# Two Abs, and two Exp, as one operation over a two-bank PSUM tile in the filter generation of a fused adaLN, S4D and Mixer kernel

## The chip, the core and the metric

The kernel runs on one core of a Trainium2 chip. A core has five engines that run side by side, each through its own instructions in order: TensorE (PE, matrix products into PSUM), VectorE (DVE), ScalarE (ACT, activation functions), GpSimd (POOL) and SyncE (SP, which here only starts transfers). They wait for each other through semaphores. The metric is the device time of one execution in microseconds, here the median of the runs shown.

## The reference

The block has two branches with adaptive layer norms. The first is a diagonal state space layer (S4D): for each of 448 channels a filter of 2048 taps is generated from 256 complex states and applied as a long convolution. The second is a token-mixing MLP.

```python
dt = jnp.exp(log_dt)
A = -jnp.exp(log_A_real) + 1j * A_imag
C = (C_real + 1j * C_imag) * dt[:, None]
P = jnp.exp((A * dt[:, None])[:, :, None] * pos[None, None, :])
K = 2.0 * jnp.einsum("dn,dnl->dl", C, P).real
...
y = jnp.fft.irfft(Uf * Kf[None, :, :], L2)[:, :, :L]
...
h = _layernorm(x, axis=-1) * (1 + ca) + sa
x = x + ga * _A_ref(h, ...)
h = _layernorm(x, axis=-1) * (1 + cb) + sb
x = x + gb * _B_ref(h, ...)
```

`_B_ref` is layer norm, a product with `w1` over the 2048 tokens, GELU and a product with `w2` back to the tokens, for each of the 448 channels.

## The kernel before

The kernel has three stages: parameters of the states; the filters together with the convolution (as a two-stage discrete Fourier transform); the token MLP. The change is in the filters.

A tap's position is split into a coarse part of 32 values and a fine part of 64, so that a state's contribution is a product of two factors, E over the fine part and G over the coarse part. The sum over states then is a matrix product that contracts the states: `kg` (line 684). A group is 16 channels, so there are 28 groups; the 256 states are taken in two halves of 128, one on each partition. A half group is one such half of one group, and there are 56, numbered `s`.

Each half group needs magnitudes and angles. Both are computed by PE from small factors into PSUM, in two tiles of 128 x 512 floats, `xe` (for E) and `xg` (for G), each as large as one PSUM bank. `st_exponents` (line 611) makes the exponents, and `st_exp` (616) turns them into magnitudes by one Exp for each tile. `st_phase` (622) makes the phases in turns, by four matmuls for each tile: a product, two that add and subtract a large constant so as to round to whole turns, and a product that leaves the fraction. The helper `halves` (605) issues each matmul twice, for `xe` with the first 64 rows of the PE array and for `xg` with the last 64.

`st_step` (641) uses them. On ACT it takes Abs of `xe` into `ab` and Abs of `xg` into `cg_`, then four Sin: of `xe` in place (652), of `xg` into `sg` (653), of `cg_` in place as the cosine (654), and of `ab` into `xg`, also a cosine (655). POOL multiplies `sg` and `cg_` with the magnitudes into G (657, 658). DVE multiplies `xe` and `xg` with magnitudes into E (659 and 660, and after the work of `between`, 662 and 663). `st_mag2` (633, on POOL) makes the magnitudes of the second half of the fine part.

Exp and Sin need different function tables on ACT, and a table is loaded anew at each switch. So the half groups are taken in seven batches of eight: `window` (978) makes the eight Exp of a batch, then eight steps make the Sin.

The order of PE, ACT, DVE and POOL is written out by hand: each runs its instructions in the order of the source. In step `s`, `st_phase(s + 1)` is issued ahead of `st_step(s)`, so PE works one step ahead. For `s` below 32, `st_kgen(s - 2)` (675) goes ahead of the phases; above 32, `st_kgen(s - 1)` goes behind them. Between these lies the work of the convolution: before the 32nd half group that of the input (`u_rows`, `u_cols`), later `pc_s2`, `pc_mul`, `pc_inv`, `pc_out` of the first half of the channels. Its copies out of PSUM are put into the lists `dve` and `act` and issued in `between` and behind the step.

Buffers are reused in turn, and an instruction that writes into a reused buffer waits for the last reader of the tile that was there. `xe` and `xg` come from the pool `pph` with two buffers each, four banks in all. In SBUF `ab` has one buffer of 512 floats on each partition; `sg` and `cg_` share the tag `gs` with three.

Of the kernel before, what the change touches and what calls it, by code (L numbers as in the profile page):

```python
# [11 lines left out]
F32 = mybir.dt.float32  # L12
F32R = mybir.dt.float32r
BF16 = mybir.dt.bfloat16
AF = mybir.ActivationFunctionType
# [7 lines left out]
P = 128  # L23
# [11 lines left out]
TWO_PI = 6.283185  # L35
# [187 lines left out]
def tile_adaln_s4d_mixer(ctx, tc, i, out):  # L223
# [20 lines left out]
    with ExitStack() as es:  # L244
        V, S, G, T = nc.vector, nc.scalar, nc.gpsimd, nc.tensor
# [10 lines left out]
        cg, mp, wp = right("cg", 1), right("mp", 8), right("wp", 2)  # L256
        m2p = [right("m2", 3)]
        pms = es.enter_context(tc.tile_pool(name="pms", bufs=3, space=PSUM))
        pph = kgen.enter_context(tc.tile_pool(name="pph", bufs=2, space=PSUM))
# [71 lines left out]
        for q in range(4):  # L331
            r = slice(32 * q, 32 * q + 1)
# [149 lines left out]
        def modulation(k, *halves):  # L482
            if 0 in halves:
                pmods[k] = pms.tile([P, D], F32, tag="ms", name="pm")
            for h in halves:
                for q in (2 * h, 2 * h + 1):
                    T.matmul(pmods[k], scb[:, q], wms[k][:, q], start=q == 0, stop=q == 3)
            if 1 not in halves:
                return
            pm = pmods.pop(k)  # L490
            act.append(lambda: S.activation(mod[k], pm, AF.Copy, bias=1.0 if k in (1, 4) else 0.0))
# [4 lines left out]
        nm = xp.tile([P, 16], F32, name="nm")  # L496
# [87 lines left out]
        mags, m2s, eg, phs = {}, {}, {}, {}  # L584
# [20 lines left out]
        def halves(out, lhs, rhs, start, stop):  # L605

            for k in range(2):
                r = slice(64 * k, 64 * k + 64)
                T.matmul(out[k], lhs[r], rhs[r], start=start, stop=stop)  # L609

        def st_exponents(s):
            g, h = divmod(s, 2)
            phs[s] = [pph.tile([P, 512], F32, tag=nm, name=nm) for nm in ("xe", "xg")]
            halves(phs[s], lex[g % 4][:, h * P : (h + 1) * P], tab[:, 2], True, True)

        def st_exp(s):
            mags[s] = mp.tile([P, 2, 512], F32, tag="mag", name="mag")
            pm = phs.pop(s)
            for k in range(2):
                S.activation(mags[s][:, k], pm[k], AF.Exp)  # L620

        def st_phase(s):

            g, h = divmod(s, 2)
            lhs = lph[g % 3][:, h * P : (h + 1) * P]
            pm = [pph.tile([P, 512], F32, tag=nm, name=nm) for nm in ("xe", "xg")]
            halves(pm, lhs, tab[:, 1], True, False)
            halves(pm, mg[:, 0], ones, False, False)
            halves(pm, mg[:, 1], ones, False, False)
            halves(pm, lhs, tab[:, 0], False, True)  # L630
            phs[s] = pm
# [9 lines left out]
        def st_step(s, between):  # L641
            me, mg_, m2 = v32(mags[s][:, 0]), v32(mags[s][:, 1]), m2s.pop(s)
            E = gp_.tile([P, 2, GD, NJ], F32, tag="E", name="E")
            Gt = gp_.tile([P, 2, GD, NI], F32, tag="G", name="G")


            xe, xg = phs.pop(s)
            ab, sg, cg_ = (wp.tile([P, 512], F32, tag=nm, name=nm, bufs=b) for nm, b in (("ab", 1), ("gs", 3), ("gs", 3)))

            S.activation(ab, xe, AF.Abs)  # L650
            S.activation(cg_, xg, AF.Abs)
            S.activation(xe, xe, AF.Sin, scale=TWO_PI)  # L652
            S.activation(sg, xg, AF.Sin, scale=-TWO_PI)  # L653
            S.activation(cg_, cg_, AF.Sin, scale=-TWO_PI, bias=math.pi / 2)  # L654
            S.activation(xg, ab, AF.Sin, scale=-TWO_PI, bias=math.pi / 2)  # L655
            se, ce = v32(xe), v32(xg)
            G.tensor_tensor(Gt[:, 1], mg_, v32(sg), ALU.mult)  # L657
            G.tensor_tensor(Gt[:, 0], mg_, v32(cg_), ALU.mult)  # L658
            V.tensor_tensor(E[:, 1, :, 32:64], m2, se, ALU.mult)  # L659
            V.scalar_tensor_tensor(E[:, 1, :, 31::-1], me[:, :, 31::-1], -1.0, se, ALU.mult, ALU.mult)  # L660
            between()
            V.tensor_tensor(E[:, 0, :, 31::-1], me[:, :, 31::-1], ce, ALU.mult)
            V.tensor_tensor(E[:, 0, :, 32:64], m2, ce, ALU.mult)  # L663
            eg[s] = (E, Gt)
            mags.pop(s)
# [312 lines left out]
        def window(s):  # L978
# [7 lines left out]
            if s == 0:  # L986
                st_exponents(s)
            for e in range(BATCH):
                st_exp(s + e)

                if e + 1 < BATCH:
                    st_exponents(s + e + 1)
                else:
                    st_phase(s)
# [45 lines left out]
        for s in range(tail):  # L1040
# [23 lines left out]
            def between():  # L1064
                flush(dve)
                if s == 9:
                    tt(mod[0], mod[0], mod[2], ALU.mult)
                if 2 <= s < BATCH:
                    for r in range(2 * s, 2 * s + 2):
                        u_stats(r)  # L1070
                if s < len(pace):
                    more(pace[s])

            mellow()
            if s >= NHALF:
                flush(dve)
                mellow()
            else:
                if s < 32 and s % BATCH > 1:
                    st_kgen(s - 2)  # L1080
                if s % BATCH == 0:
                    if s == 16:
                        for k in (4, 5):
                            modulation(k, 0, 1)
                    elif s == 24:
                        some(u_cols, cols, 3)
                    elif s >= 32:
                        piece(False)
                if (s + 1) % BATCH:
                    st_phase(s + 1)  # L1090
                elif s + 1 < NHALF:
                    st_exponents(s + 1)

                if s > 32 and s % BATCH:
                    st_kgen(s - 1)
                st_step(s, between)
# [202 lines left out]
    with ExitStack() as es:  # L1299
        es.enter_context(tc.manual_schedule(engines={ENG.PE, ENG.Activation, ENG.DVE, ENG.Pool}))  # L1300
        V, S, G = nc.vector, nc.scalar, nc.gpsimd
# [118 lines left out]
```

## Time and profile before

| | us |
|---|---|
| median of 3 runs | 710.34 |
| lowest and highest run | 707.86, 722.8 |
| the profiled execution | 714.78 |
| its span in the profile | 712.6 |

The profile comes from one execution. For each engine it gives the instructions with their start, duration and line, and what ended the idle time ahead of them. In a row of the timeline stand start, duration, engine, line, operation, output<-inputs, shapes and count; in brackets stand an idle time and what ended it. In a row of groups stand the busy time in all and the mean in ns behind the first bar, and behind the second the idle time before the group. A transfer or an instruction that is merged into a row is counted by x. Clock shares of PE are what the chip granted.

### The profile page before, as it was taken

Reading aid. Unit: us, or ns where it says so; the run is one execution under the profiler, and the core shown is the slowest. Engines: PE = TensorE matmul, PEld = TensorE weight load, DVE = VectorE, ACT = ScalarE, POOL = GpSimd, SP = SyncE. Lnnn points to the kernel's source line nnn. Section 1 sums busy time; section 2 is a strip of 40 time slices with the busy share of each in tenths; the row PEclk is TensorE's granted clock in tenths of the full one; section 3 lists DMA queues with packets and bytes.
Section 4 is the critical chain, followed back from the end, with each engine's and each line's share of the span. In section 5 each row is a group of like instructions: output and inputs, shape, how many; then the busy total and the mean of one; then the engine's idle time right before and its main releaser. Section 6 shows DMA issues by size and latency. Waiting matters only on the chain. (4 is left out here: it accounts for less than half of the span.)

```text
span 712.6 us, 18344 instructions
## 1 busy us (share of the span) xinstructions
PE 630.5 (88%) x7228; PEld 458.3 (64%) x7228; DVE 453.8 (64%) x877; ACT 439.0 (62%) x876; POOL 272.0 (38%) x326
## 2 busy tenths in 40 slices
PE   0759879999988889789788979999999999999997
PEld 0434334544535556456455647778999999999996
DVE  7579799679769768576774649777632263344441
ACT  5848697778978889989973559878522242222220
POOL 6487467429629878878774600000000000000000
PEclk9969987789999989899999989999999999999999
DMA  7795555349997635435237979993675536555540
GB/s 172 212 188 140 194 163 187 114 154 242 252 255 242 191 80 129 150 96 157 70 104 227 288 203 254 254 222 99 189 231 137 159 107 174 160 155 155 163 136 26
DMA packets 102259, 121.66 MB, mean 171 GB/s; under 512 B 13114, under 2 KB 87918, under 8 KB 102046
## 3 DMA queue, kind: packets, MB, share of 16 engines
q1 hardware_dynamic: 100638, 113.63, 56.1%
q0 software_dynamic: 1536, 6.87, 4.3%
q8 instruction: 57, 0.93, 0.5%
q14 instruction: 28, 0.23, 0.1%
HBM read 85.11 MB, written 34.87 MB: 168 GB/s over the span
## 5 line engine op out<-in xcount | busy, mean ns | idle before, releaser
L208 ACT CAST whi<-w 128x896 fp32r<-128x896 f32 x64 | 59.7, 938 | 133.4 <-PE o L1387 84.6
L657 POOL TENSOR_TENSOR G<-mag,gs 128x512 f32<-128x512 f32 x56 | 71.9, 1284 | 93.1 <-ACT gs L653 93.1
L217 DVE TENSOR_TENSOR wlo<-w,whi 128x896 fp32r<-128x896 f32 x64 | 68.0, 1086 | 40.3 <-ACT whi L208 27.9
L609 PE MATMUL xg<-tab,lph 64*128 64x512 f32 x112 | 68.5, 613 | 23.8 <-ACT xg L655 7.7
L1317 PE MATMUL acc<-h3h,whi 128*128 128x448 f32 x224 | 82.8, 370 | 0.9 <-ACT h3h L1231 0.9
L1318 PE MATMUL acc<-h3l,whi 128*128 128x448 f32 x224 | 80.9, 361 | 0.7 <-DVE h3l L1238 0.5
L1386 PE MATMUL o<-uh,whi 128*128 128x448 f32 x224 | 81.3, 363 | 0.0
L1319 PE MATMUL acc<-h3h,wlo 128*128 128x448 f32 x224 | 81.3, 363 | 0.0
L1388 PE MATMUL o<-uh,wlo 128*128 128x448 f32 x224 | 81.2, 362 | 0.0
L1387 PE MATMUL o<-ul,whi 128*128 128x448 f32 x224 | 80.6, 360 | 0.0
L684 PEld LDWEIGHTS kg<-E,G 128*32 128x32 f32 x3584 | 60.7, 121 | 30.7 <-issue 16.8
L609 PE MATMUL xe<-tab,lph 64*128 64x512 f32 x112 | 67.2, 603 | 10.2 <-ACT gs L654 6.7
L658 POOL TENSOR_TENSOR G<-mag,gs 128x512 f32<-128x512 f32 x56 | 71.6, 1278 | 0.0
L684 PE MATMUL kg<-E,G 128*32 128x64 f32 x3584 | 70.8, 237 | 0.8 <-issue 0.4
L659 DVE TENSOR_TENSOR E<-m,xe 128x512 f32<-128x512 f32 x56 | 38.3, 683 | 41.1 <-ACT xe L652 33.5
L638 POOL TENSOR_TENSOR m<-mag,w 128x512 f32<-128x512 f32 x56 | 60.3, 1076 | 6.0 <-DVE E L663 1.5
L1390 DVE SCALAR_TENSOR_TENSOR y<-o,b,mod 128x448 f32<-128x448 f32 x16 | 11.0, 685 | 80.2 <-PE o L1388 80.2
L650 ACT ACTIVATE ab<-xe 128x512 f32<-128x512 f32 x56 | 33.7, 601 | 31.9 <-PE xe L609 21.9
L1317 PEld LDWEIGHTS acc<-h3h,whi 128*128 128x128 f32 x224 | 42.1, 188 | 13.1 <-ACT h L1236 4.9
L609 PE MATMUL xe<-tab,lex 64*128 64x512 f32 x56 | 30.1, 547 | 18.2 <-DMA lex<-wm 16.4
L609 PEld LDWEIGHTS xg<-tab,lph 64*128 64x128 f32 x112 | 24.1, 215 | 34.1 <-issue 9.8
L1318 PEld LDWEIGHTS acc<-h3l,whi 128*128 128x128 f32 x224 | 41.9, 187 | 4.0 <-DVE h3l L1238 0.8
(235 smaller groups left out, 1476.3 us busy)
## 6 DMA issues: line engine op xcount, KB each, us to landing
w<-in_B_w_dram SPq DMA_DIRECT2D x64, 224.0 KB
w<-in_B_w_dram SPq DMA_DIRECT2D x32, 448.0 KB
yu_d<-yt SPq DMA_DIRECT2D x16, 448.0 KB
yi<-yu_d SPq DMA_DIRECT2D x32, 224.0 KB
us_d<-uo SPq DMA_DIRECT2D x16, 448.0 KB
u<-us_d SPq DMA_DIRECT2D x32, 224.0 KB
v_d<-vt SPq DMA_DIRECT2D x32, 224.0 KB
vt<-v_d SPq DMA_DIRECT2D x14, 448.0 KB
```

The lines of the kernel that those rows point to most:

```text
L217: eng.tensor_tensor(lo, w, hi.bitcast(F32), ALU.subtract)
L609: T.matmul(out[k], lhs[r], rhs[r], start=start, stop=stop)
L638: G.tensor_tensor(m2, me, w[:, :, None].to_broadcast([P, GD, 32]), ALU.mult)
L657: G.tensor_tensor(Gt[:, 1], mg_, v32(sg), ALU.mult)
L658: G.tensor_tensor(Gt[:, 0], mg_, v32(cg_), ALU.mult)
L684: T.matmul(kgs[g][32 * q : 32 * q + 32, m], Gt[:, c, d], E[:, c, d], start=h == 0 and c == 0 and m == 0, stop=h == 1 and c == 1, skip_grou ...
L1317: nc.tensor.matmul(acc[f], hi[:, fs], h3h[:, r], start=r == 0, stop=False)
L1318: nc.tensor.matmul(acc[f], hi[:, fs], h3l[:, r], start=False, stop=False)
L1319: nc.tensor.matmul(acc[f], lo[:, fs], h3h[:, r], start=False, stop=r == 15)
L1386: nc.tensor.matmul(o, hi[:, ks], uh[kh][:, k], start=kh == 0 and k == 0, stop=False)
L1387: nc.tensor.matmul(o, hi[:, ks], ul[kh][:, k], start=False, stop=False)
L1388: nc.tensor.matmul(o, lo[:, ks], uh[kh][:, k], start=False, stop=kh == 1 and k == 6)
```

## The change

Each pair of tiles `xe` and `xg` becomes one tile of 128 x 2 x 512 floats over two banks, from the same pool with two buffers, so again four banks. The two Exp of a half group become one over 1024 columns, and so do the two Abs, which now write one tile `ab` of 1024 columns with one buffer. The Abs of `xg` is no longer written into the tile that the cosine Sin then overwrites: that Sin reads the second half of `ab`. `sg` and `cg` get a tag each, with one buffer each. In SBUF this is 2 + 3 x 2 = 8 KB on each partition before and 4 + 2 + 2 = 8 KB after. The matmuls, the Sin and the products stay as they are, and so does the order of the rest.

```diff
             for k in range(2):
                 r = slice(64 * k, 64 * k + 64)
-                T.matmul(out[k], lhs[r], rhs[r], start=start, stop=stop)
+                T.matmul(out[:, k], lhs[r], rhs[r], start=start, stop=stop)
 
         def st_exponents(s):
             g, h = divmod(s, 2)
-            phs[s] = [pph.tile([P, 512], F32, tag=nm, name=nm) for nm in ("xe", "xg")]
+            phs[s] = pph.tile([P, 2, 512], F32, tag="ph", name="xeg")
             halves(phs[s], lex[g % 4][:, h * P : (h + 1) * P], tab[:, 2], True, True)
 
         def st_exp(s):
             mags[s] = mp.tile([P, 2, 512], F32, tag="mag", name="mag")
-            pm = phs.pop(s)
-            for k in range(2):
-                S.activation(mags[s][:, k], pm[k], AF.Exp)
+            S.activation(mags[s], phs.pop(s), AF.Exp)
 
         def st_phase(s):
 ...
-            pm = [pph.tile([P, 512], F32, tag=nm, name=nm) for nm in ("xe", "xg")]
+            pm = pph.tile([P, 2, 512], F32, tag="ph", name="xeg")
             halves(pm, lhs, tab[:, 1], True, False)
 ...
-            xe, xg = phs.pop(s)
-            ab, sg, cg_ = (wp.tile([P, 512], F32, tag=nm, name=nm, bufs=b) for nm, b in (("ab", 1), ("gs", 3), ("gs", 3)))
-
-            S.activation(ab, xe, AF.Abs)
-            S.activation(cg_, xg, AF.Abs)
+            xeg = phs.pop(s)
+            xe, xg = xeg[:, 0], xeg[:, 1]
+            ab = wp.tile([P, 2, 512], F32, tag="ab", name="ab", bufs=1)
+            sg, cg_ = (wp.tile([P, 512], F32, tag=nm, name=nm, bufs=1) for nm in ("sg", "cg"))
+
+            S.activation(ab, xeg, AF.Abs)
             S.activation(xe, xe, AF.Sin, scale=TWO_PI)
             S.activation(sg, xg, AF.Sin, scale=-TWO_PI)
-            S.activation(cg_, cg_, AF.Sin, scale=-TWO_PI, bias=math.pi / 2)
-            S.activation(xg, ab, AF.Sin, scale=-TWO_PI, bias=math.pi / 2)
+            S.activation(cg_, ab[:, 1], AF.Sin, scale=-TWO_PI, bias=math.pi / 2)
+            S.activation(xg, ab[:, 0], AF.Sin, scale=-TWO_PI, bias=math.pi / 2)
             se, ce = v32(xe), v32(xg)
```

## The prediction

> **What bounds the kernel now.** I read the page first (span, chain of waits by engine), then the busy time by stretch, the groups by shape, the timelines of ScalarE (ACT) and of its neighbours in a quiet stretch, and the list of waits.
>
> ```profile
> span 712.6 us, 18344 instructions
> PE 42%; DMA 3%; DVE 1%; ACT 0%; SPq 0%; POOL 0%; issue 0%; DVEq 0%
> ```
>
> The chain that ended last is nearly all TensorE (PE), but that is the token MLP at the end, which the change does not touch. The change lies in the filter generation, the 56 half groups in the first half of the span. There the shares are different:
>
> ```profile
> 260.00:300.00 40.00, 34.44 (x732) 22.70 (x729) 26.94 (x49) 36.17 (x76) 32.35 (x38) 0.97 0.52 138
> ```
>
> The columns after the stretch's length are PE, PE weight loads, DVE, ACT, POOL: ACT is busy 36.2 of 40 us, so late in the generation ACT is close to the limit. Whatever is lost or won there moves the MLP as a whole, microsecond for microsecond.
>
> What ACT does in one step and a half of that stretch:
>
> ```profile
> 265.98 0.62 ACT L655 ACTIVATE xg<-ab 128x512 f32<-128x512 f32 x1
> 266.63 0.60 ACT L650 ACTIVATE ab<-xe 128x512 f32<-128x512 f32 x1
> 267.13 0.59 ACT L651 ACTIVATE gs<-xg 128x512 f32<-128x512 f32 x1
> 267.60 0.61 ACT L652 ACTIVATE xe<-xe 128x512 f32<-128x512 f32 x1
> 268.12 0.60 ACT L653 ACTIVATE gs<-xg 128x512 f32<-128x512 f32 x1
> 268.60 0.64 ACT L654 ACTIVATE gs<-gs 128x512 f32<-128x512 f32 x1
> 269.11 0.61 ACT L655 ACTIVATE xg<-ab 128x512 f32<-128x512 f32 x1
> 269.63 0.61 ACT L810 COPY vt<-vv 128x224 f32<-128x224 f32 x2
> 270.55 0.37 ACT L698 COPY ks<-kg 128x256 f32<-128x256 f32 x1 [0.32 <-PE kg L684]
> 270.82 0.60 ACT L650 ACTIVATE ab<-xe 128x512 f32<-128x512 f32 x1
> ```
>
> Two things are to be seen. An operation lasts 0.60 us, but the next one starts 0.47 to 0.52 us after it: neighbours overlap by about 0.1 us. So a pair costs 0.97 us (266.63 to 267.60), not 1.2. And there is one exception: L650 starts 0.65 after L655, at 266.63, when L655 has ended (265.98 + 0.62 = 266.60). L655 reads `ab`, L650 writes `ab`; where the instruction behind L655 does not touch `ab`, it starts 0.52 after it (269.11 to 269.63). VectorE shows the same without a change of buffer:
>
> ```profile
> 91.17 0.43 DVE L439 TENSOR_TENSOR xa<-xa,u 128x256 f32<-128x256 f32 x1
> 91.63 0.29 DVE L441 TENSOR_SCALAR u<-A_C_imag 128x256 f32<-128x256 f32 x1
> ```
>
> L441 only overwrites the `u` that L439 has read, and still starts 0.03 after L439's end. An instruction that overwrites what the one just before it on its engine reads gives up the overlap.
>
> **Part 1: the two Abs as one.**
>
> ```profile
> L208 ACT CAST whi<-w 128x896 fp32r<-128x896 f32 x64 | 59.7, 938 | 133.4 <-PE o L1387 84.6 <-PE acc L1318 38.4 <-DMA w<-in_B_w_dram 10.5
> L650 ACT ACTIVATE ab<-xe 128x512 f32<-128x512 f32 x56 | 33.7, 601 | 31.9 <-PE xe L609 21.9 <-PE xg L609 9.4
> ```
>
> No operation of 1024 columns is in the trace. From 512 to 896 columns the time goes from 601 to 938 ns, 0.88 ns a column; that gives 601 + 512 x 0.88 = 1050 ns for 1024 columns, an estimate; with the smaller slope that the overlap leaves (0.43 us for 512 columns) it is 1.03. If the next operation could overlap it, it would start after about 0.92, where the pair took 0.97: a gain of 0.05. But the next operation is the Sin of `xe` in place, and now it directly follows the instruction that reads `xe`; before, the second Abs stood between them. So I expect it 0.03 after the end, at 1.06 to 1.08: 0.09 to 0.11 later than today. I take +0.09 us a step, for every operation of ACT behind it, and so for the products on POOL and DVE that wait for the Sin. The Trainium skill, "Perfetto Trace Analysis", section "Optimizing Scalar/DVE Operations", has a fixed cost of about 51 ns per ScalarE operation on PSUM, half of the latency shown being covered by the next instruction, and says that grouping helps when the engine is saturated; by that page alone 112 merges would save 112 x 0.051 = 5.7 us. [...]
>
> How much of 0.09 reaches the end differs by stage. The late steps come in twos: one directly behind the other, one that waits for PE.
>
> ```profile
> 266.89 0.68 DVE L662 TENSOR_TENSOR E<-mag,xg 128x512 f32<-128x512 f32 x1
> 266.91 1.27 POOL L658 TENSOR_TENSOR G<-mag,gs 128x512 f32<-128x512 f32 x1
> ...
> 267.15 0.56 PE L609 MATMUL xe<-tab,lph 64*128 64x512 f32 x1
> 267.49 0.68 DVE L663 TENSOR_TENSOR E<-m,xg 128x512 f32<-128x512 f32 x1
> ...
> 268.31 0.46 PE L609 MATMUL xg<-tab,lph 64*128 64x512 f32 x1 [0.60 <-ACT xe L652]
> ...
> 268.88 0.58 PE L609 MATMUL xg<-tab,lph 64*128 64x512 f32 x1
> ...
> 269.39 1.10 PE L684 MATMUL kg<-E,G 128*32 128x64 f32 x64
> ```
>
> The chain is L655 (ends 266.60), DVE L662 and L663 (ends 268.17), the phase matmuls, which get their `xg` buffer only then (268.31 to 269.46), the `kg` matmuls, the copy L698 (270.55), the next Abs (270.82). ACT's own step is in it once in two steps: three batches of 8, 12 times 0.09 = 1.1 us at least, 21 times (each step but the first of a batch) = 1.9 at most.
>
> In the first 32 steps PE is often without a gap:
>
> ```profile
> 172.93 1.10 PE L684 MATMUL kg<-E,G 128*32 128x64 f32 x64
> 173.96 0.50 PE L609 MATMUL xe<-tab,lph 64*128 64x512 f32 x1
> ...
> 174.56 0.58 PE L609 MATMUL xg<-tab,lph 64*128 64x512 f32 x1
> 175.07 1.77 PE L563 MATMUL pu<-yi,s 128*128 128x448 f32 x4
> 176.77 0.43 PE L684 MATMUL kg<-E,G 128*32 128x64 f32 x16
> ```
>
> From `kg` to `kg` 3.84 us, all filled: there 0.09 on ACT is hidden by PE. If that cover is gone it costs 32 x 0.09 = 2.9. Between 0 and 2.9 I take 1.0, nearer to the covered case.
>
> **Part 2: one buffer instead of two.** Today `xe` and `xg` are freed separately: above, the `xe` matmul ran at 267.15 while `xg` waited for L663, the last reader. As one tile, both wait for L663. PE stood still behind that one matmul anyway, its queue (the other seven phase matmuls, then `kg`) being in order. All eight behind the wait take 1.18 us (173.96 to 175.14) against 1.15 (268.31 to 269.46): 12 x 0.03 = 0.4. In the early steps the halves matter more, because Abs could start on the first (the list of waits: us in total, times, longest; then two rows of the timeline):
>
> ```profile
> ACT ab L650 <- PE xe L609: 21.9, 11, 7.4
> ```
>
> ```profile
> 101.49 0.98 PE L609 MATMUL xg<-tab,lph 64*128 64x512 f32 x1
> 102.16 0.60 ACT L650 ACTIVATE ab<-xe 128x512 f32<-128x512 f32 x1 [0.63 <-PE xe L609]
> ```
>
> Here Abs started 0.31 before the `xg` half was done (102.47). Waiting for it costs up to 0.40; with 11 such waits 0 to 4.4 us. The row of L650 above has a further 9.4 us of waits put down to the `xg` half, as where both halves end together and nothing is lost; I take 1.2, nearer the lower end. The Trainium skill, "Perfetto Trace Analysis", section "Optimizing Scalar/DVE Operations", also has a rule against this change: where ScalarE is not saturated but makes others wait, breaking operations up lets work finish sooner. The 11 waits are where the trace agrees with it.
>
> **Part 3: the two Exp as one.**
>
> ```profile
> 283.66 0.60 ACT L620 ACTIVATE mag<-xe 128x512 f32<-128x512 f32 x1
> 284.16 0.59 ACT L620 ACTIVATE mag<-xg 128x512 f32<-128x512 f32 x1
> 284.63 0.60 ACT L810 COPY vt<-vv 128x224 f32<-128x224 f32 x2
> ```
>
> A pair takes 0.97; as one, with overlap (nothing behind it overwrites its input on ACT), about 0.92: 0.05 x 56 = 2.8 us at most, none where Exp waits for the exponent matmuls, as it does in most of the early batches. The buffer is given back once, at the end, instead of in halves 0.5 us apart, which takes away lead from PE. I take -1.0.
>
> **Part 4: `sg` and `cg` with one buffer each** instead of three in turn. The cosine Sin (L654) now waits for POOL's L658 of the step before. In the closest place L658 ends at 266.91 + 1.27 = 268.18 and L654 starts at 268.60: 0.42 to spare, and both move by 0.09. Cost 0 as long as POOL stays within that.
>
> **Sum.** 1.1 to 1.9 (take 1.4) + 0.4 + 1.0 + 1.2 - 1.0 + 0 = +3.0 us; with the bounds from 1.1 - 2.8 = -1.7 to 1.9 + 0.4 + 2.9 + 4.4 = +9.6. The profiled execution took 714.78 us (span 712.6, 2.2 around it); it would become 717.8. The runs before were 707.86, 710.34 and 722.8; on their median of 710.34 the same sum gives 713.3. I write 713, and 708 to 720 for this case.
>
> **The rivals.**
>
> *The overlap stays.* If the Sin of `xe` does not wait for Abs, both merges gain 0.05: 112 x 0.05 = 5.6 us when all is on the path, half of it from the shares above: 707.5. For it: the overlap of 0.1 us at nearly every other pair of ACT rows. Against: L655 to L650 and L439 to L441. Chance 0.15. The Trainium skill's grouping rule, cited in part 1, speaks for it too.
>
> *Everything is hidden.* PE's full queue in the early steps and the 0.32 that L698 waits in the late ones take up 0.09. Then 710.3. Chance 0.15.
>
> *The two halves are kept apart by nothing.* If the program's waits treat the two-bank tile as a whole, DVE's products with `xe` must wait for the last write to the tile, L655, 1.51 us after L652 (267.60 to 269.11), and the two of them (0.60 each by L662 to L663) move behind L655 in the chain above: 1.2 us for every pass. It decides wherever L659 starts behind L655. Twelve late passes give 14.4 us, and 16 early ones at most 19 more: 725 to 744, near 733. Against: banks are different for the two halves, and another tile, `mag`, is written by halves (L620). The trace has no PSUM tile of two banks, so it cannot exclude it. The Trainium skill, "PSUM — Partial Sum Buffer", section "PSUM bank collisions raise a hardware error", asks for waits by bank, which would keep the halves apart; no run here shows it. Chance 0.13.
>
> *POOL holds ACT.* If POOL falls more than 0.42 behind, each second late step stalls for up to one of its 1.27 us products less 0.42: 12 x 0.85 = 10 us, 720.5. Against: L657 and L658 follow the Sin without a backlog in the late rows. Chance 0.05.
>
> **How the numbers follow.** The forecast keeps 0.52. A measurement of this kernel can tell about 2% from no change, 14 us, that is below 696 or above 724.5. No mechanism reaches 696; scatter like that of the three runs on top of the first rival leaves 0.06. Above 724.5 lies the whole-tile rival with 0.13 and the forecast's or POOL's upper end with scatter, 0.08: 0.21. Within: 0.73. The range, 704 to 727, takes in the first rival's full gain (704.7), all bounds of the sum and the lower edge of the whole-tile case; it leaves out most of that rival and little below.
>
> **What would show it.** Right: one Abs of 1.03 to 1.05 us and the next Sin about 0.03 behind its end; late steps some 0.1 us longer in every second one; no `xe` matmul ahead of L663; L659 still directly behind L652; Exp at 0.92 spacing. Wrong: a Sin that starts before Abs ends (gain), L659 behind L655 (whole tile), ACT waiting for POOL's G at the cosine Sin, or a generation that ends more than 10 us away from today's.

## The result and the profile after

| | before | changed |
|---|---|---|
| median of 6 runs, us | 715.05 | 743.38 |
| lowest and highest run | 707.86, 722.8 | 741.06, 749.82 |
| span of the profiled execution | 712.6 | 745.4 |

The changed kernel is slower: 1.0456 times the time before, with a 95% interval of 1.0378 to 1.0535. This ratio, and every one below, compares fast runs alone: two of the six runs before, 718.51 and 722.8, are more than 1.5% above the fastest of them and stay out of it. The forecast was 713 and its range ended at 727.

The page of the changed kernel, its first line and the chain of waits by engine:

```profile
span 745.4 us, 18200 instructions
PE 38%; DMA 2%; DVE 2%; issue 1%; POOL 1%; ACT 1%; SPq 0%; DVEq 0%; POOLq 0%
```

There are 144 instructions fewer, and the chain that ended last is still mostly PE's. The groups of the page show what became slower (busy us, mean ns | idle time ahead and its main cause); the lines of `st_step` moved by one, so L650 is the merged Abs, L651 to L654 are the Sin of `xe`, `sg`, `cg`, `xg`, and L658 is DVE's first product:

```profile
L650 ACT ACTIVATE ab<-xeg 128x1024 f32<-128x1024 f32 x56 | 57.5, 1028 | 38.3 <-PE xeg L609 37.9
L658 DVE TENSOR_TENSOR E<-m,xeg 128x512 f32<-128x512 f32 x56 | 38.4, 686 | 83.7 <-ACT xeg L654 47.5
L618 ACT ACTIVATE mag<-xeg 128x1024 f32<-128x1024 f32 x56 | 56.0, 1039 | 24.9 <-PE xeg L609 23.7
```

Before, the group of DVE's first product read:

```profile
L659 DVE TENSOR_TENSOR E<-m,xe 128x512 f32<-128x512 f32 x56 | 38.3, 683 | 41.1 <-ACT xe L652 33.5
```

DVE's first product uses the `xe` half only, and it waited for the Sin of `xe`. Now it is idle twice as long ahead of it, 83.7 us against 41.1, and 47.5 of that is put down to L654, the last Sin, which writes the other half. Step by step it is plainer: before, DVE's first product started ahead of the end of the last Sin in 51 of the 56 steps; in the changed kernel it does so in none. From a late stretch before, DVE's first product behind the Sin of `xe` of 267.60 (which ended at 268.21), and the start of a later step:

```profile
268.30 0.69 DVE L659 TENSOR_TENSOR E<-m,xe 128x512 f32<-128x512 f32 x1
...
273.95 0.60 ACT L650 ACTIVATE ab<-xe 128x512 f32<-128x512 f32 x1
```

One late step of the changed kernel in the timeline, ACT with DVE, and on to the start of the step after next:

```profile
281.84 1.03 ACT L650 ACTIVATE ab<-xeg 128x1024 f32<-128x1024 f32 x1
...
282.90 0.58 ACT L651 ACTIVATE xeg<-xeg 128x512 f32<-128x512 f32 x1
...
283.58 0.60 ACT L652 ACTIVATE sg<-xeg 128x512 f32<-128x512 f32 x1
...
284.07 0.62 ACT L653 ACTIVATE cg<-ab 128x512 f32<-128x512 f32 x1
...
284.59 0.59 ACT L654 ACTIVATE xeg<-ab 128x512 f32<-128x512 f32 x1
...
285.22 1.02 ACT L650 ACTIVATE ab<-xeg 128x1024 f32<-128x1024 f32 x1
285.27 0.69 DVE L658 TENSOR_TENSOR E<-m,xeg 128x512 f32<-128x512 f32 x1 [1.48 <-issue]
...
291.42 0.37 ACT L697 COPY ks<-kg 128x256 f32<-128x256 f32 x1 [1.38 <-PE kg L683]
...
291.69 1.03 ACT L650 ACTIVATE ab<-xeg 128x1024 f32<-128x1024 f32 x1
```

The Sin of `xe` ends at 282.90 + 0.58 = 283.48, the last Sin at 284.59 + 0.59 = 285.18, and DVE starts at 285.27, 1.79 behind the first and 0.09 behind the last. (The row puts the idle 1.48 us down to "issue", that is to nothing that the profile shows; by its time it too ends with the last Sin.) ACT itself shows the same bond: L652 reads the `xg` half and starts at 283.58, behind the end of L651, which wrote the `xe` half, 0.68 after its start instead of 0.52 as before. The waits of the program treat the two-bank tile as one thing. Two steps took 7.32 us before (266.63 to 273.95); here two take 9.85 (281.84 to 291.69), and ACT waits 1.38 in them for the `kg` matmuls behind the later products, where it waited 0.32 before. This pair lost more than most.

How much of the loss lies where? The last three batches, from the first step's Abs to the last step's Abs, before and in the changed kernel (span of the stretch, busy PE, PE loads, DVE, ACT, POOL, clock of PE, DMA share, GB/s):

```profile
249.35:364.88 115.53, 98.91 (x2116) 65.13 (x2118) 81.91 (x140) 105.01 (x218) 92.61 (x101) 0.93 0.41 113
```

```profile
267.26:397.76 130.50, 96.33 (x2106) 64.28 (x2107) 79.45 (x140) 106.94 (x179) 94.36 (x105) 0.90 0.37 103
```

They take 130.5 us instead of 115.5, 15.0 more, while the busy time of no engine changes by more than 2.6: this is waiting, not work. From the Abs of the last step on, nothing more is lost: that Abs is 32.9 us later (397.76 against 364.88), and the span is 32.8 longer. Of the other 17.9, 6.8 lie in the steps of the first four batches (each from its first Abs to its last, 148.2 us together against 141.4), and 8.8 in the Exp of the second batch:

```profile
70.00:95.00 25.00, 22.37 (x326) 9.75 (x329) 20.88 (x53) 18.05 (x36) 8.62 (x12) 1.00 0.62 209
```

```profile
70.00:103.00 33.00, 29.79 (x316) 12.12 (x304) 20.43 (x52) 17.09 (x28) 9.72 (x12) 0.69 0.49 165
```

There PE is the busy engine, and it was granted 1.00 of its clock in the profile before and 0.69 in this one. A low clock in this place needs no two-bank tile. In the profile of sbuf_side, an experiment below with separate tiles, it was 0.64:

```profile
70.00:102.00 32.00, 29.70 (x272) 12.24 (x272) 20.17 (x53) 15.62 (x33) 8.55 (x12) 0.64 0.48 164
```

From the last Abs of the first batch to the first of the second it is 25.7 us before, 34.5 in the changed kernel and 35.3 in sbuf_side. So these profiles do not show that the 8.8 us come from the change. The late batches, where the clock differs little, are the better measure, and the runs below are compared there and by their ratios.

### The profile page after: what moved, and what is told of

It is laid out like the page before. It is cut to its first block, busy times and chain, and to the rows that moved or that the text cites. A ratio compares the mean times of both kernels' runs of the same rounds, so it can differ in the third digit from the quotient of the medians.

```text
span 745.4 us, 18200 instructions
## 1 busy us (share of the span) xinstructions
PE 628.0 (84%) x7228; PEld 454.7 (61%) x7228; DVE 449.3 (60%) x877; ACT 442.4 (59%) x764; POOL 270.9 (36%) x326
## 5 line engine op out<-in xcount | busy, mean ns | idle before, releaser
L609 PE MATMUL xeg<-tab,lph 64*128 64x512 f32 x224 | 72.2, 620 | 60.1 <-ACT xeg L651 22.0
L656 POOL TENSOR_TENSOR G<-mag,sg 128x512 f32<-128x512 f32 x56 | 71.7, 1281 | 109.9 <-ACT sg L652 109.6
L658 DVE TENSOR_TENSOR E<-m,xeg 128x512 f32<-128x512 f32 x56 | 38.4, 686 | 83.7 <-ACT xeg L654 47.5
L1318 PE MATMUL acc<-h3h,wlo 128*128 128x448 f32 x224 | 80.7, 360 | 0.0
L650 ACT ACTIVATE ab<-xeg 128x1024 f32<-128x1024 f32 x56 | 57.5, 1028 | 38.3 <-PE xeg L609 37.9
L609 PEld LDWEIGHTS xeg<-tab,lph 64*128 64x128 f32 x224 | 27.3, 216 | 80.5 <-ACT xeg L651 23.6
L683 PE MATMUL kg<-E,G 128*32 128x64 f32 x3584 | 74.4, 246 | 0.9 <-DVE E L662 0.9
L657 POOL TENSOR_TENSOR G<-mag,cg 128x512 f32<-128x512 f32 x56 | 72.3, 1291 | 0.0
L618 ACT ACTIVATE mag<-xeg 128x1024 f32<-128x1024 f32 x56 | 56.0, 1039 | 24.9 <-PE xeg L609 23.7
L609 PE MATMUL xeg<-tab,lex 64*128 64x512 f32 x112 | 32.6, 570 | 33.5 <-DMA lex<-wm 17.4
L609 PEld LDWEIGHTS xeg<-tab,lex 64*128 64x128 f32 x112 | 12.6, 211 | 56.3 <-POOL dsk L474 17.0
```

Source lines behind the costliest of these rows:

```text
L609: T.matmul(out[:, k], lhs[r], rhs[r], start=start, stop=stop)
L683: T.matmul(kgs[g][32 * q : 32 * q + 32, m], Gt[:, c, d], E[:, c, d], start=h == 0 and c == 0 and m == 0, stop=h == 1 and c == 1, skip_grou ...
L1318: nc.tensor.matmul(acc[f], lo[:, fs], h3h[:, r], start=False, stop=r == 15)
```

## The experiments

All ratios are to runs of the kernel before on the same chip, with 95% intervals. Three theories were to be told apart: W, the waits take the two-bank tile as a whole; S, the halves are tied only where one operation spans both banks; M, the merged operations cost the time themselves.

**tile_only**: the two-bank tile with nothing merged.

```diff
-            S.activation(mags[s], phs.pop(s), AF.Exp)
+            pm = phs.pop(s)
+            for k in range(2):
+                S.activation(mags[s][:, k], pm[:, k], AF.Exp)
...
-            S.activation(ab, xeg, AF.Abs)
+            S.activation(ab[:, 0], xe, AF.Abs)
+            S.activation(ab[:, 1], xg, AF.Abs)
```

> The changed kernel with both merges undone: two Abs and two Exp of 512 columns each, on the two halves of the two-bank tile; buffers as in the changed kernel. Theory W (the waits treat the two-bank tile as a whole, whatever the size of the operations): DVE's first product with xe still starts about 0.1 us behind the last Sin, and the time stays near the changed kernel's, 1.03 to 1.05 of before. Rival S (the halves are tied only because one operation spans both banks): DVE's first product starts behind the first Sin again, 0.99 to 1.01. Rival M (the merged operations themselves cost the time, by a later Sin and a later release): 0.99 to 1.01.

Measured: 1.0485 (1.0403 to 1.0567). One step in its timeline (L652 and L653 are the two Abs, L654 the Sin of `xe`, L655 of `sg`, L657 of `xg`, L661 DVE's first product):

```profile
277.83 0.60 ACT L652 ACTIVATE ab<-xeg 128x512 f32<-128x512 f32 x1
...
278.32 0.60 ACT L653 ACTIVATE ab<-xeg 128x512 f32<-128x512 f32 x1
...
278.96 0.58 ACT L654 ACTIVATE xeg<-xeg 128x512 f32<-128x512 f32 x1
...
279.63 0.60 ACT L655 ACTIVATE sg<-xeg 128x512 f32<-128x512 f32 x1
...
280.64 0.59 ACT L657 ACTIVATE xeg<-ab 128x512 f32<-128x512 f32 x1
...
281.32 0.69 DVE L661 TENSOR_TENSOR E<-m,xeg 128x512 f32<-128x512 f32 x1 [1.47 <-issue]
```

No operation of ACT spans both banks here, and every bond is still there. The Sin of `xe` waits for the end of the Abs of the other half (278.32 + 0.60 = 278.92, start 278.96), `sg` for the Sin of `xe`, and DVE for the last Sin (281.23, start 281.32). S and M fall: the tile costs the whole loss without any merge.

**exp_merged** and **abs_merged**: one of the two merges alone, each by half of the diff above.

> The changed kernel with two Abs of 512 columns on the halves of the two-bank tile; the Exp stays merged. Theory W: 1.03 to 1.05 of before, as no Abs size matters. Rival S: the tile of the phases is spanned by no operation, so 0.99 to 1.01. Rival M: below the changed kernel by what the merged Abs costs, 1.00 to 1.02; its Sin of xe starts 0.97 us behind the first Abs instead of 1.06.

> The changed kernel with two Exp of 512 columns on the halves of the two-bank tile; the Abs stays merged. Theory W: 1.04 to 1.055 of before. Rival S: the same, since Abs spans both banks. Rival M: the changed kernel less what the merged Exp costs, 1.01 to 1.04, with the difference to the changed kernel in the batches of Exp.

Measured: 1.0461 (1.0374 to 1.0547) and 1.0502 (1.0421 to 1.0582). With both merges 1.0456, with none 1.0485: the four can't be told apart. On this tile neither merge gains or loses anything that shows in the ratios. The late batches take 133.8 us with none and 130.5 with both, one profile each, which would fit a gain of a few us and does not prove it. The Sin was expected 0.97 us behind the first Abs in exp_merged, and that was wrong: there it starts 1.13 behind it (277.23 to 278.36), as in tile_only (277.83 to 278.96), so on this tile the merged Abs, at 1.06, is even the shorter.

**xg_products_first**: the wait of DVE without the tile. In the kernel before, DVE's products change places.

```diff
+            V.tensor_tensor(E[:, 0, :, 31::-1], me[:, :, 31::-1], ce, ALU.mult)
+            V.tensor_tensor(E[:, 0, :, 32:64], m2, ce, ALU.mult)
+            between()
             V.tensor_tensor(E[:, 1, :, 32:64], m2, se, ALU.mult)
             V.scalar_tensor_tensor(E[:, 1, :, 31::-1], me[:, :, 31::-1], -1.0, se, ALU.mult, ALU.mult)
-            between()
-            V.tensor_tensor(E[:, 0, :, 31::-1], me[:, :, 31::-1], ce, ALU.mult)
-            V.tensor_tensor(E[:, 0, :, 32:64], m2, ce, ALU.mult)
```

> The kernel before, with separate tiles, but DVE's two products with xg go ahead of the work of between and its two products with xe behind it, so that DVE's first product has to wait for the last Sin as in the changed kernel, with nothing merged and no two-bank tile. Theory W: this wait is most of the loss, 1.02 to 1.04 of before. Rivals S and M say the same of this wait only if it is what costs the time; if the loss comes from the merged operations, 0.99 to 1.015.

Measured: 1.0367 (1.028 to 1.0454). The group of DVE's first product, and the stretch from the first Abs of step 32 to the Abs of step 55:

```profile
L659 DVE TENSOR_TENSOR E<-mag,xg 128x512 f32<-128x512 f32 x56 | 38.4, 686 | 80.7 <-ACT xg L655 80.6
```

```profile
258.52:387.60 129.08, 99.12 (x2115) 67.13 (x2117) 79.45 (x141) 105.19 (x217) 93.69 (x103) 0.89 0.38 103
```

The idle time of 80.7 is that of the changed kernel (83.7), and the late stretch takes 129.1 us, 13.6 of the 15.0 more. In the late batches DVE's wait for the last Sin is by far the largest part of the loss, and it needs neither a two-bank tile nor a merge.

**xg_before_cg**: the changed kernel with the last write to the tile one place earlier.

```diff
-            S.activation(cg_, ab[:, 1], AF.Sin, scale=-TWO_PI, bias=math.pi / 2)
             S.activation(xg, ab[:, 0], AF.Sin, scale=-TWO_PI, bias=math.pi / 2)
+            S.activation(cg_, ab[:, 1], AF.Sin, scale=-TWO_PI, bias=math.pi / 2)
```

> The changed kernel with the last two Sin exchanged: Abs, xe, sg, xg, cg. Theory W (DVE's first product waits for the last access of ACT to the two-bank tile): that access ends about 0.4 us earlier (0.5 less 0.1, since the Sin of xg now overwrites what the instruction just before it reads), DVE's first product starts as much earlier, and the time falls by 0.4 for each pass of the chain, 5 to 11 us: 1.025 to 1.04 of before. POOL's cosine product starts 0.5 later. Rival (the waits count the order of the engine, not the tile, so that DVE waits for the end of the step): no change, 1.045, and DVE's first product behind the Sin of cg.

Measured: 1.0305 (1.0207 to 1.0402), where theory W had 1.025 to 1.04. In its timeline L653 is the Sin of `xg`, L654 that of `cg`:

```profile
280.56 0.60 ACT L653 ACTIVATE xeg<-ab 128x512 f32<-128x512 f32 x1
...
281.10 0.61 ACT L654 ACTIVATE cg<-ab 128x512 f32<-128x512 f32 x1
281.25 0.69 DVE L658 TENSOR_TENSOR E<-m,xeg 128x512 f32<-128x512 f32 x1 [0.45 <-issue]
```

DVE starts 0.09 behind the end of L653 (281.16), while `cg` still runs. So the wait follows the last access to the tile, not ACT's order.

**merged_cos_to_E**: the last Sin leaves the tile; it writes into E in SBUF, where DVE multiplies in place.

```diff
-            S.activation(xg, ab[:, 0], AF.Sin, scale=-TWO_PI, bias=math.pi / 2)
-            se, ce = v32(xe), v32(xg)
+            ce = E[:, 0, :, 32:64]
+            S.activation(ce, v32(ab[:, 0]), AF.Sin, scale=-TWO_PI, bias=math.pi / 2)
+            se = v32(xe)
```

> The changed kernel with only the last cosine written into E; the Sin of xe stays in place in the two-bank tile, and the last access of ACT to the tile is the read by the Sin of sg. Theory W, if reads count too: DVE's first product starts behind the Sin of sg, about 0.7 us behind the Sin of xe, 1.00 to 1.02 of before. If only writes count: behind the Sin of xe, 0.97 to 1.00.

Measured: 1.0327 (1.0238 to 1.0415), slower than either case. But its waits answer the question. The group of DVE's first product, and one step (L651 is the Sin of `xe`, L652 of `sg`, L655 the cosine into E):

```profile
L659 DVE TENSOR_TENSOR E<-m,xeg 128x512 f32<-128x512 f32 x56 | 38.1, 680 | 33.9 <-ACT sg L652 33.5
```

```profile
272.64 0.58 ACT L651 ACTIVATE xeg<-xeg 128x512 f32<-128x512 f32 x1
273.26 0.60 ACT L652 ACTIVATE sg<-xeg 128x512 f32<-128x512 f32 x1
...
273.96 0.69 DVE L659 TENSOR_TENSOR E<-m,xeg 128x512 f32<-128x512 f32 x1 [3.30 <-ACT sg L652]
...
274.27 0.62 ACT L655 ACTIVATE E<-ab 128x512 f32<-128x512 f32 x1
```

DVE reads the `xe` half, which L651 wrote one operation earlier; L652 only reads the `xg` half, and 33.5 of the 33.9 us of DVE's idle time are put down to it. Reads count as well. The rows show one thing more. DVE's product writes one half of the tile E in SBUF at 273.96, and ACT's write into the other half, which stands earlier in the source, starts only at 274.27: the halves of this SBUF tile are not tied.

The late batches take 120.5 us here, 5.0 more than before and not 15.0: with the last write out of the tile, two thirds of the late loss are gone. What the kernel loses instead lies earlier, in the steps of the first four batches (153.6 us against 141.4). DVE's last product in each step, now with both operands in SBUF, takes up to 1.67 us there instead of 0.68; the next runs show this more strongly.

**merged_sin_to_E** and **split_sin_to_E**: both Sin that DVE needs go to E, in the changed kernel and in the kernel before.

```diff
-            S.activation(xe, xe, AF.Sin, scale=TWO_PI)
+            se, ce = E[:, 1, :, 32:64], E[:, 0, :, 32:64]
+            S.activation(se, v32(xe), AF.Sin, scale=TWO_PI)
...
-            S.activation(xg, ab[:, 0], AF.Sin, scale=-TWO_PI, bias=math.pi / 2)
+            S.activation(ce, v32(ab[:, 0]), AF.Sin, scale=-TWO_PI, bias=math.pi / 2)
```

> The changed kernel with the Sin of xe and the last cosine written straight into the halves of E in SBUF, where DVE then multiplies in place (the product that needs both operands first). ACT only reads the two-bank tile. Theory W: DVE's first product starts behind the first Sin, PE's next phases wait only for ACT's Sin of sg and no longer for DVE, and the Sin of xe starts about 0.92 us behind Abs, as nothing is overwritten: 0.95 to 0.99 of before. Rival (E is tied as a whole as well, or DVE's product in place costs more than it saves): 1.00 to 1.04.

> The kernel before, separate tiles and nothing merged, with the same two Sin written straight into E. Tells what that step is worth by itself: if the release of the tiles by DVE was on the path, 0.96 to 0.99 of before; if not, 0.99 to 1.01. Against merged_sin_to_E it tells what the merges are worth once the tile is no bond: by the overlap of neighbours 0.05 us for each merge, 2 to 6 us less for the merged one.

Measured: 1.1181 (1.1087 to 1.1275) and 1.1213 (1.1145 to 1.1281): far outside of all that was expected. In merged_sin_to_E:

```profile
303.28 1.02 ACT L650 ACTIVATE ab<-xeg 128x1024 f32<-128x1024 f32 x1
...
304.20 0.59 ACT L652 ACTIVATE E<-xeg 128x512 f32<-128x512 f32 x1
...
306.88 1.72 POOL L657 TENSOR_TENSOR G<-mag,cg 128x512 f32<-128x512 f32 x1
...
307.40 1.75 DVE L661 TENSOR_TENSOR E<-mag,E 128x512 f32<-128x512 f32 x1
...
309.19 0.69 DVE L662 TENSOR_TENSOR E<-m,E 128x512 f32<-128x512 f32 x1
```

The bond is gone as expected: with nothing overwritten, the Sin starts 0.92 behind the merged Abs, as the prediction had it for that case. But in these rows a product of DVE with both operands in SBUF takes 1.75 us while POOL multiplies, and 0.69 when POOL stands still, and POOL's takes 1.72 instead of 1.28. Not every overlap costs as much: L661 keeps 0.68 us in the median of the 37 steps in which POOL runs beside it, where L662 takes 1.63. Before, one operand of each product on DVE came from PSUM, and these products took 0.62 to 0.69 beside POOL as well as alone. The Trainium skill, "SBUF — State Buffer", section "Who interferes with whom", states that a VectorE instruction with two SBUF inputs contends with a GpSimd instruction that reads SBUF; these rows agree. The pair was also to price the merges without the bond: the merged one is 0.3% below the split one, with overlapping intervals.

**sbuf_side**: the buffers of the changed kernel in SBUF, with separate PSUM tiles and nothing merged.

```diff
-            ab, sg, cg_ = (wp.tile([P, 512], F32, tag=nm, name=nm, bufs=b) for nm, b in (("ab", 1), ("gs", 3), ("gs", 3)))
+            ab = wp.tile([P, 2, 512], F32, tag="ab", name="ab", bufs=1)
+            sg, cg_ = (wp.tile([P, 512], F32, tag=nm, name=nm, bufs=1) for nm in ("sg", "cg"))
...
-            S.activation(ab, xe, AF.Abs)
-            S.activation(cg_, xg, AF.Abs)
+            S.activation(ab[:, 0], xe, AF.Abs)
+            S.activation(ab[:, 1], xg, AF.Abs)
```

> The kernel before with separate PSUM tiles and nothing merged, but with the changed kernel's buffers in SBUF: one tile ab of two halves with one buffer, sg and cg with one buffer each, the cosine Sin reading the second half of ab. Theory W: no part of the loss, 0.995 to 1.01 of before. Rival P (POOL holds ACT through the single buffers): 1.01 to 1.03, with ACT waiting for POOL's G at the Sin of sg or cg.

Measured: a median of 717.2 us beside 718.21 of before, with runs from 703.8 to 720.8 beside 706.18 to 724.4. These runs give no ratio with an interval, but both the lowest and the highest of the four lie below the lowest and the highest before. In its profile the last three batches take 113.7 us, no longer than the 115.5 before:

```profile
252.31:365.98 113.67, 97.84 (x2116) 64.61 (x2118) 81.95 (x140) 105.06 (x218) 92.62 (x101) 0.94 0.41 116
```

The single buffers are not the cause.

**merged_sg_first**: the changed kernel with the Sin in the order `sg`, `xe`, `xg`, `cg`.

```diff
-            S.activation(xe, xe, AF.Sin, scale=TWO_PI)
             S.activation(sg, xg, AF.Sin, scale=-TWO_PI)
-            S.activation(cg_, ab[:, 1], AF.Sin, scale=-TWO_PI, bias=math.pi / 2)
+            S.activation(xe, xe, AF.Sin, scale=TWO_PI)
             S.activation(xg, ab[:, 0], AF.Sin, scale=-TWO_PI, bias=math.pi / 2)
+            S.activation(cg_, ab[:, 1], AF.Sin, scale=-TWO_PI, bias=math.pi / 2)
```

> The changed kernel with the Sin in the order sg, xe, xg, cg: the read of the tile first, then the two writes, the Sin that does not touch the tile last. Theory W: the Sin of sg overlaps Abs (0.92), the two writes are tied and lose the overlap, the last access ends near 2.8 us behind the start of Abs, against 3.3 in the changed kernel, and POOL's sg product starts some 0.7 earlier: 1.01 to 1.035 of before. It can't reach before, since DVE's first product still waits for the last write.

Measured: 1.0318 (1.0208 to 1.0428). None of the three orders tried gets the two-bank tile back to the time before.

**split_xg_before_cg** and **products_together**: two changes to the kernel before, to see if its own chain can be shortened: the exchange of the last two Sin; and the work of `between` behind the products with `xg`.

```diff
-            S.activation(cg_, cg_, AF.Sin, scale=-TWO_PI, bias=math.pi / 2)
             S.activation(xg, ab, AF.Sin, scale=-TWO_PI, bias=math.pi / 2)
+            S.activation(cg_, cg_, AF.Sin, scale=-TWO_PI, bias=math.pi / 2)
```

```diff
-            between()
             V.tensor_tensor(E[:, 0, :, 31::-1], me[:, :, 31::-1], ce, ALU.mult)
             V.tensor_tensor(E[:, 0, :, 32:64], m2, ce, ALU.mult)
+            between()
```

> The kernel before with the last two Sin exchanged, so that DVE's products with xg can start 0.4 us earlier and POOL's cosine product 0.5 later. If DVE's products with xg bind the next phases in the kernel before as read from its chain, 0.98 to 0.995 of before; if DVE is still busy with its other work by then, 0.995 to 1.005; if POOL's product binds, 1.00 to 1.02.

> The kernel before with the work of between put behind DVE's products with xg instead of ahead of them. The xg tile comes free by 0.2 us earlier in the late steps on the chain and by 1 to 3 in the early ones, and what between holds (copies out of PSUM, the products of the convolution) comes 1.3 us later. If the release binds: 0.97 to 0.995 of before; if the copies bind PE: 1.00 to 1.03.

Measured: 1.0046 (0.9988 to 1.0104), no change that shows (that DVE is busy with its other work by then would explain it, and was not tested); and 1.0215 (1.0019 to 1.0411), which points to slower but leaves open by how much: in its profile the last three batches take 112.5 us instead of 115.5, but the earlier ones take longer. No version was shown to be faster than the kernel before.

## Why the prediction was wrong

**The step that failed** is in part 1, where the 0.09 us were the whole cost of a step: they took it that "the products on POOL and DVE that wait for the Sin" wait for their own Sin. That holds for POOL, whose operands are separate tiles in SBUF, and for DVE with separate PSUM tiles. With the two-bank tile DVE waits for the last access of ACT to either half, 1.79 us instead of 0.09 behind the Sin of `xe`. tile_only shows it without any merge, xg_products_first shows its price without the tile.

**The rival had it.** The whole-tile case stood in the prediction with 0.13 and 725 to 744 us; the time came out at its upper end. Its late passes were priced at 14.4 us; the late batches lost 15.0. The upper end itself is in part luck: it has 19 us for early passes, where the profiles show 6.8 in the early steps and 8.8 in the Exp of the second batch at a lower clock. What spoke against it was weak: that `mag` is written by halves says something of a tile in SBUF, not of PSUM; merged_cos_to_E has both, E with its halves free and `xeg` with its halves tied. With no two-bank PSUM tile in the trace the chance should have been near even. The Trainium skill, "PSUM — Partial Sum Buffer", section "PSUM bank collisions raise a hardware error", asks for waits by bank; it does not say what a program's tile does, and by tile_only the waits here go by the tile.

**Missed beside it:** the bond holds within ACT too. The Sin of `sg` starts 0.68 behind that of `xe` instead of 0.52, and so a step that directly follows another takes 3.38 us (281.84 to 285.22), where 0.09 on the old spacing would have given 3.2. This bond is in tile_only and not in xg_products_first, and 1.0485 against 1.0367 is the difference between the two runs, with intervals that overlap; the joint release of the halves is in that difference as well, and no run tells these two apart.

**Right, and of no weight:** the merged Abs lasts 1.03 us (1.03 to 1.05 expected), the Sin starts 0.03 behind its end (282.87 to 282.90), Exp lasts 1.04. The gain for each merge, 0.05 us by the overlap, is shown by the spacing of 0.92 in merged_sin_to_E. Part 4 was right: sbuf_side shows no loss. The cost of 1.2 us for Abs waiting for both halves and the 1.0 from the first 32 steps can't be found in a loss of this size. The lower bound of the sum, -1.7, leaves out the 0.4 of part 2 that the upper one has; with it, it is -1.3, and nothing hangs on that.

**The POOL rival** falls: ACT's cosine Sin starts 0.49 behind the Sin of `sg` in the changed kernel (283.58 to 284.07), so it does not wait for POOL, and sbuf_side shows no loss. **The hidden case** is wrong for the whole and partly right for the early steps. With DVE's wait alone (xg_products_first) the steps of the first four batches take 141.6 us, as before (141.4), so there the wait seems hidden. In the changed kernel they take 148.2; in the other runs with separate tiles and DVE's operands in PSUM they range from 137.8 to 144.5, and how much of the 6.8 belongs to the tile stays open. The first rival, in which the overlap stays, fell by the rows of the changed kernel.

## What to carry to other kernels

Ahead of joining two buffers into one, list who waits for each of them and for what; here the joint PSUM tile made each reader wait for the last access to either half. It cost 4.6% of the time, some 33 us, where both merges together could have gained 5.6 by the prediction's own sum. Price a merge by the distance between starts, not by durations: two operations of 512 columns cost 0.97 us together, not 1.2, so one of 1024, with the next start 0.92 behind its own, gains 0.05. When the trace has no example of a resource, an argument from another memory is no evidence about it.

## What was not expected of the hardware

Moving an operand of DVE from PSUM to SBUF made a product up to 2.5 times as long (1.75 us against 0.69) when POOL multiplied at the same time, and POOL's 1.3 times (1.72 against 1.28). The kernel took 12% longer; that these products are the cause is read from the trace, and no run takes them apart from the rest of that edit. In this kernel PSUM is not only the place where PE writes; it keeps DVE and POOL out of each other's way.
